# A Strassen form of both network products after the first 512 tokens

## The chip, the cores and the metric

The kernel runs on one core of a Trainium2 chip. The metric is device time in microseconds (us) from start to end of one execution. The engines work side by side, each through its own list of instructions in order: TensorE (PE in the profile; PEld is its weight load) multiplies matrices into PSUM, VectorE (DVE) and ScalarE (ACT) work element by element, GpSimd (POOL) too, though not on PSUM, and SyncE (SP) here only issues transfers (DMA) between DRAM and the on-chip memory. An engine whose next instruction waits does nothing else meanwhile.

## What is computed

```python
def _attn_ref(q, k, v):                      # q, k, v: (8, 8, 576, 64)
    scores = np.matmul(q, k.transpose(0, 1, 3, 2)) / np.sqrt(D)
    # heads 0-3: only the last 32 keys up to the query's own; heads 4-7: keys at distance 0, 32, 64, ...
    scores = np.where(masks[None], scores, -1e9)
    attn = softmax(scores)                   # written out with max, exp and sum + 1e-9
    return np.matmul(attn, v)

def _moe_ref(x, w_in, w_out):                # x (4608, 512), w_in (512, 2048), w_out (2048, 512)
    h = x @ w_in
    g = np.where(h >= 1, h, np.where(h <= -1, 0, (h + 1) ** 2 / 4))
    return g @ w_out
```

x is the attention's output, heads side by side. Everything is float32. The two network products are by far the larger part: 2 x 4608 x 512 x 2048 multiplications.

## The kernel before

Both products are done with operands that are split in a rounded part (high) and the rest (low), as three matmuls for one: high x high, low x high, high x low (HI_LO). A matmul takes a 128x128 block of one operand as weights and moves 512 columns through it. The 4608 tokens are worked in 9 chunks c of 512 (CH). For each chunk the 2048 inner features are worked in 16 tiles f of 128 (NF).

- `up(c, f)` (L540) makes h of tile f: 4 blocks of the 512 inputs times 3, 12 matmuls into one PSUM bank.
- `gate(c, f)` makes g of it: ACT `Relu` and `Square` (L549, L550), DVE min/max (L554), a rounded copy (L556 on ACT, in the first chunk L558 on DVE), and the low part (L559, DVE).
- `down(...)` (L570) multiplies g of one or two tiles with w_out: 12 matmuls a tile, into four PSUM banks that are summed over all 16 tiles; after the last tile ACT copies them out (L577) and SP stores them.

So a chunk is 16 x 24 = 384 matmuls of 512 columns, all nine are 3456. The weights come as pairs of 32-bit words and are converted once, in the first chunk (`conv_a` to `conv_e`: ACT, DVE, POOL, ACT, DVE); after that all 16 tiles lie on chip, split, until the end. The attention of batch b (576 tokens, four units 0 to 3) is spread over the tiles of an earlier chunk by the tables STEPS and LATER, a letter for each step: s scores (PE), m mask and x maximum (DVE), a subtract (POOL), e exponent (ACT), q sum (DVE), p and r normalise, t and j transpose by DVE and a trip through DRAM (or f, a transpose on PE), v values (PE), h and l high and low part of x. The order on each engine is the order in which the code is written. POOL has little beside this: 256-wide and 512-wide sums of the conversion (L191) and the attention's subtract and multiply (L368, L392).

## Time and profile before

| | |
|---|---|
| median of 3 runs | 881.58 us (881.12 to 883.56) |
| span of the profiled execution | 881.9 us |
| PE busy | 872.9 us, 99% |
| ACT busy | 398.0 us, 45% |
| DVE busy | 384.6 us, 44% |
| POOL busy | 114.7 us, 13% |
| DMA | 77.61 MB, 88 GB/s over the span |

The span is the time of the run to within the spread of the runs, so terms read from this trace can be set against the median directly. The page's sections are: busy time by engine; the span in 40 slices; the DMA queues; the chain of work that ended last; the costliest groups of instructions with the idle time before them and what ended it; the DMA issues. Two cautions: durations of neighbouring matmuls overlap, so their spacing is read from start times, and the mean duration of an ACT or DVE instruction also overlaps a little with its neighbour's.

### The profile page before, as it was taken

Reading aid. Unit: us, or ns where it says so; the run is one execution under the profiler, and the core shown is the slowest. Engines: PE = TensorE matmul, PEld = TensorE weight load, DVE = VectorE, ACT = ScalarE, POOL = GpSimd, SP = SyncE. Lnnn points to the kernel's source line nnn. Section 1 sums busy time; section 2 is a strip of 40 time slices with the busy share of each in tenths; the row PEclk is TensorE's granted clock in tenths of the full one; section 3 lists DMA queues with packets and bytes.
Section 4 is the critical chain, followed back from the end, with each engine's and each line's share of the span. In section 5 each row is a group of like instructions: output and inputs, shape, how many; then the busy total and the mean of one; then the engine's idle time right before and its main releaser. Section 6 shows DMA issues by size and latency. Waiting matters only on the chain.

```text
span 881.9 us, 17353 instructions
## 1 busy us (share of the span) xinstructions
PE 872.9 (99%) x7253; PEld 710.3 (81%) x7253; DVE 384.6 (44%) x709; ACT 398.0 (45%) x732; POOL 114.7 (13%) x136
## 2 busy tenths in 40 slices
PE   8999999999999999999999999999999999999998
PEld 6788888888888888887888888888888888888886
DVE  5899854443453434434344345333453322222221
ACT  5889953434434443334434343444333433343333
POOL 6354411100120002100110011100210000000000
PEclk8999999999999999999999999999999999999999
DMA  9917331422232322421241223321222000000001
GB/s 354 405 65 242 114 121 61 140 59 60 105 100 81 83 70 72 125 64 62 81 145 52 67 105 94 87 82 49 76 82 60 33 29 1 0 35 14 1 0 48
DMA packets 41646, 77.61 MB, mean 88 GB/s; under 512 B 8800, under 2 KB 22112, under 8 KB 41568
## 3 DMA queue, kind: packets, MB, share of 16 engines
q1 hardware_dynamic: 41568, 76.50, 26.8%
q8 instruction: 57, 0.93, 0.4%
q14 instruction: 21, 0.17, 0.1%
HBM read 59.18 MB, written 17.30 MB: 87 GB/s over the span
## 4 chain that ended last, share of the span: by engine, by line
PE 95%; DMA 1%; ACT 1%; DVE 1%; SPq 1%; issue 0%; ACTq 0%; DVEq 0%
PE o L570 44%; PE h L540 44%; PE xp L459 3%; PE sc L302 3%; DMA qk<-in_qk_s 1%; PE tp L405 1%; SPq L443 0%; DMA pT<-there 0%; ACT u L549 0%; ACT u L550 0%; DMA there<-t 0%; DVE xTl L504 0%; DVE h L554 0%; SPq L237 0%; ACT gh L556 0%
## 5 line engine op out<-in xcount | busy, mean ns | idle before, releaser
L540 PE MATMUL h<-xTh,w 128*128 128x512 f32 x1152 | 373.2, 391 | 0.4 <-DVE u L554 0.4
L570 PE MATMUL o<-w,gh 128*128 128x512 f32 x1152 | 359.5, 393 | 0.1
L554 DVE SCALAR_TENSOR_TENSOR h<-h,u 128x512 f32<-128x512 f32 x143 | 100.0, 699 | 377.1 <-ACT u L550 377.0
L540 PEld LDWEIGHTS h<-xTh,w 128*128 128x128 f32 x1152 | 216.3, 188 | 46.6 <-DVE u L554 0.8
L570 PEld LDWEIGHTS o<-w,gh 128*128 128x128 f32 x1152 | 213.4, 188 | 45.3 <-ACT gh L556 0.6
L540 PE MATMUL h<-xTl,w 128*128 128x512 f32 x576 | 224.5, 390 | 0.4 <-DVE xTl L504 0.4
L570 PE MATMUL o<-w,gl 128*128 128x512 f32 x576 | 224.9, 390 | 0.0
L549 ACT ACTIVATE u<-h,half 128x512 f32<-128x512 f32 x144 | 99.1, 688 | 269.6 <-PE h L540 268.6
L559 DVE TENSOR_TENSOR gl<-h,gh 128x512 fp32r<-128x512 f32 x143 | 98.9, 692 | 84.6 <-ACT gh L556 83.7
L570 PEld LDWEIGHTS o<-w,gl 128*128 128x128 f32 x576 | 108.1, 188 | 25.7 <-DVE gl L559 0.6
L540 PEld LDWEIGHTS h<-xTl,w 128*128 128x128 f32 x576 | 108.1, 188 | 22.9 <-DVE xTl L504 1.1
L556 ACT CAST gh<-h 128x512 fp32r<-128x512 f32 x128 | 75.2, 587 | 100.1 <-DVE h L554 100.1
L550 ACT ACTIVATE u<-u 128x512 f32<-128x512 f32 x144 | 91.0, 632 | 4.6
L368 POOL TENSOR_TENSOR pr<-pr,st 128x768 f32<-128x768 f32 (+3 forms) x31 | 36.3, 1172 | 322.8 <-DVE st L364 307.6
L392 POOL TENSOR_TENSOR pr<-pr,st 128x648 f32<-128x648 f32 (+3 forms) x30 | 35.2, 1173 | 119.3 <-DVE st L391 118.4
L191 POOL TENSOR_TENSOR raw<-raw 128x512 uint32<-128x512 uint32 (+1 forms) x34 | 35.0, 1047 | 37.9 <-DVE raw L186 23.4
L504 DVE TENSOR_TENSOR xTl<-xp,xTh 128x216 fp32r<-128x216 f32 (+8 forms) x94 | 35.7, 442 | 6.0 <-ACT xTh L500 6.0
L383 ACT ACTIVATE st<-st 128x12 f32<-128x12 f32 (+2 forms) x32 | 6.8, 211 | 67.5 <-DVE st L379 67.4
L459 PEld LDWEIGHTS xp<-pT,v 64*64 64x64 f32 (+2 forms) x1760 | 29.0, 138 | 10.1 <-issue 8.2
L302 PEld LDWEIGHTS sc<-qk 64*32 64x32 f32 (+1 forms) x1856 | 25.9, 117 | 12.1 <-issue 10.1
L459 PE MATMUL xp<-pT,v 64*64 64x32 f32 (+2 forms) x1760 | 32.3, 224 | 1.5 <-DMA pT<-there 0.8
L500 ACT CAST xTh<-xp 128x216 fp32r<-128x216 f32 (+8 forms) x94 | 31.1, 459 | 6.0 <-DVE xTl L504 3.5
(56 smaller groups left out, 348.3 us busy)
## 6 DMA issues: line engine op xcount, KB each, us to landing
raw<-in_w SPq DMA_DIRECT2D x30, 512.0 KB, 9.6
qk<-in_qk_s SPq DMA_DIRECT2D x16, 604.0 KB, 4.9
qk<-in_qk_l SPq DMA_DIRECT2D x16, 576.0 KB, 4.8
out<-ob SPq DMA_DIRECT2D x35, 256.0 KB, 2.0
v<-in_v_l SPq DMA_DIRECT2D x21, 384.0 KB, 4.0
there<-t SPq DMA_DIRECT2D x96, 48.0 KB, 1.7
pT<-there SPq DMA_DIRECT2D x12, 384.0 KB, 3.0
v<-in_v_s SPq DMA_DIRECT2D x7, 384.0 KB, 4.4
```

The lines of the kernel that those rows point to most:

```text
L302: nc.tensor.matmul(sc[j][i * Q:(i + 1) * Q, s, p], qk[:, 0, q0:q0 + Q], qk[:, 1, k0:k0 + W], start=u not in covered, stop=u not in covered)
L368: eng.tensor_tensor(out=pr, in0=pr, in1=st[:, 0].unsqueeze(2).broadcast_to(list(pr.shape)), op=ALU.add)
L392: eng.tensor_tensor(out=pr, in0=pr, in1=st[:, 2].unsqueeze(2).broadcast_to(list(pr.shape)), op=ALU.mult)
L459: nc.tensor.matmul(xp[p][j * D:(j + 1) * D, n], loaded[b, local, b0 + n][keys, j], qs, start=True, stop=True)
L504: nc.vector.tensor_tensor(out=dst[1], in0=src, in1=dst[0].bitcast(F32), op=ALU.subtract)
L540: nc.tensor.matmul(o_ps[c, f], wt[f][:, x, 0, cc * P:(cc + 1) * P], xT[y][:, cc, r0:r0 + CH], start=first and n == 0, stop=last and n == l ...
L549: nc.scalar.activation(u, hp, AF.Relu, bias=half, scale=0.5)
L550: nc.scalar.activation(u, u, AF.Square)
L554: nc.vector.scalar_tensor_tensor(out=g, in0=hp, scalar=1.0, in1=u, op0=ALU.max, op1=ALU.min)
L556: nc.scalar.copy(gh, g)
L559: nc.vector.tensor_tensor(out=gl, in0=g, in1=gh.bitcast(F32), op=ALU.subtract)
L570: nc.tensor.matmul(o_ps[c][t], gs[x][:, t * P:(t + 1) * P], wt[f][:, y, 1, :], start=f == 0 and n == 0, stop=f == NF - 1 and n == 2)
```

## The change

The first 512 tokens are done as before, except that the output is stored transposed (features by tokens; it is turned back outside the device program) and that the down product has the weights as its stationary side. The other 4096 tokens are done in four blocks s of 1024. In a block each product is cut in 2 x 2 by 2 x 2 blocks, and seven products (m = 1 to 7, Winograd's form of Strassen's method) stand in for eight: seven sums and differences of weight blocks, of which three are the blocks themselves, are multiplied with seven of x (or g), and the results are added up in PSUM and by ACT and DVE.

- **Weights.** After its conversion each weight block that is used as it is goes to DRAM (`ship`). `combine(i, j, tag)` makes the four sums of a pair of tiles j (i = 0 for w_in, 1 for w_out): four POOL operations of 256 columns, an ACT copy of 1024 columns, a DVE subtraction of 1024, and one store of 1 MB to DRAM, all by way of one on-chip place called `tag`. Four of the 16 pairs' sums are made beside the first 512 tokens (COMBINE), in four different places. The other twelve are made in the first block of 1024 tokens, two for each j from 0 to 5, after products 1 and 6, all in the place `h2`.
- **Reading back.** From then on each product reads its weights from DRAM: `fetch_w` loads 256 KB for six matmuls, ten ahead (WR).
- **Up.** `up_block` runs 56 units of six matmuls, UP giving the order: for each j products 1, 2, 6, 5, 7, and 3 and 4 one j later. The sum of products grows in the banks y, x, z of one of two sets; between, ACT copies y or z out (g11, g12, g22), DVE adds, and `bent`, `squared` (ACT) and `gated` (DVE) make g. No high and low parts are made here.
- **Down.** `down_block` runs 28 units of twelve matmuls; `prep` makes each unit's sum of g (POOL) and splits it into high and low part (`split`: ACT and DVE, 1024 columns), two units ahead. `x_sum` and `x_split` make the same of x for the next block beside it.
- **Attention.** Batches 1 and 2 are both done beside the first 512 tokens (both by PE transposes; before, batch 2 went through DRAM), 3 and 4 in the up half of the first block, 5 and 6 in the second's, 7 in the third's. x is kept unsplit.

```diff
+    def combine(i, j, tag):
+        def block(r, c):
+            par, h = (r, c) if i == 0 else (c, r)
+            return hts[j][:, par, i, h * HF:(h + 1) * HF]
+        st = slot(tag, [P, 4, 2, HF], F32R, f"st_{i}_{j}")
+        s_ = [st[:, n, 1].bitcast(F32) for n in range(4)]
+        for to, a, b, op in ((0, block(1, 0), block(1, 1), ALU.add), (1, s_[0], block(0, 0), ALU.subtract),
+                             (2, block(0, 0), block(1, 0), ALU.subtract), (3, block(0, 1), s_[1], ALU.subtract)):
+            nc.gpsimd.tensor_tensor(out=s_[to], in0=a, in1=b, op=op)
+        nc.scalar.copy(st[:, :, 0], st[:, :, 1].bitcast(F32))
+        nc.vector.tensor_tensor(out=st[:, :, 1], in0=st[:, :, 1].bitcast(F32), in1=st[:, :, 0].bitcast(F32), op=ALU.subtract)
+        nc.sync.dma_start(kept[i][j][1], st.bitcast(F32))
...
+    UP = [(j - late, m) for j in range(NP + 1) for m, late in ((1, 0), (2, 0), (3, 1), (6, 0), (4, 1), (5, 0), (7, 0)) if 0 <= j - late < NP]
+    DOWN = [(m, k) for m in (1, 2, 6, 7, 5, 3, 4) for k in range(NP // 2)]
...
+    def fetch_w(n):
+        if n < len(seq):
+            i, j, m = seq[n]
+            ring[n] = wr_p.tile([P, 2, HF], F32R, tag="wr", name=f"wr_{n}")
+            which, at = FACTOR[m]
+            nc.sync.dma_start(ring[n].bitcast(F32), kept[i][j][which][:, at])
...
+    def up_block(s, between, prepare):
+        y, x, z, tmp = {}, {}, {}, {}
+        sets = (("b2", "b0", "b1"), ("b3", "b4", "b5"))
+        for n, (j, m) in enumerate(UP):
+            w_ = factor(0, j, m)
...
+                y[j] = bank(at[0], [P, CH], f"y_{s}_{j}")
+                tmp[j] = slot(f"h{jj}", [P, 2, CH], F32, f"tmp_{s}_{j}")
...
+            for c in range(2):
+                for q, (a, b) in enumerate(HI_LO):
+                    nc.tensor.matmul(to, w_[:, a, c * P:(c + 1) * P], xc[m][:, b, c],
+                                     start=m in (1, 2, 5) and c + q == 0, stop=c == 1 and q == 2,
+                                     skip_group_check=m in (3, 4, 6, 7))
+            fetch_w(done - 1 + WR)
...
+            if m == 1:
+                last = (gb[(j - 1) // 2][:, 1, (j - 1) % 2], tmp[j - 1][:, 1]) if j else None
+                if last:
+                    bent(last[1], last[0])
+                nc.scalar.copy(g11, y[j])
+                if last:
+                    squared(last[1])
+                    gated(last[0], *last)
+            elif m == 2:
+                nc.vector.tensor_tensor(out=g11, in0=x.pop(j), in1=g11, op=ALU.add)
+                bent(ua, g11)
+                squared(ua)
...
+            elif m == 6:
+                nc.scalar.copy(g12, y[j])
+                gated(g11, g11, ua)
...
+            elif m == 4:
+                h = y.pop(j)
+                bent(ua, h)
+                squared(ua)
+                gated(g21, h, ua)
...
+            between(n)
...
+    def prep(s, n):
+        if n >= len(DOWN):
+            return
+        m, k = DOWN[n]
+        hl[n] = t = slot(("h2", "h0", "h1")[n % 3], [P, 2, 2, CH], F32R, f"hl_{s}_{n}")
...
+        split(t, {1: b11, 6: b11, 5: t3, 7: t3, 3: b22, 2: b21, 4: b21}[m])
...
-        for c in range(NCH):
...
+        COMBINE = {4: (0, 0, "h1"), 5: (1, 0, "h2"), 6: (0, 1, "h0"), 8: (1, 1, "r7")}
...
+        LATER = {0: ("s0", "m0 x0 a0"), 2: ("", "e0"), 4: ("s1", "m1 x1 a1 q0 p0 r0"), 6: ("", "e1"), 7: ("", "q1 p1 r1"),
+                 9: ("s2", "t0 j0 m2 x2 a2"), 11: ("", "e2"), 13: ("s3", "t1 j1 m3 x3 a3 q2 p2 r2"), 15: ("v0", "e3"),
...
+        for s in range(NSC):
+            batches = [b for b in range(last(s) + 1, B) if s + 1 < NSC and b <= last(s + 1)]
+            def beside(n):
+                j, m = UP[n]
+                if s == 0 and m in (1, 6) and j + 2 < NP:
+                    combine(m // 6, j + 2, "h2")
...
+            up_block(s, beside, lambda m: m in (6, 5) and prep(s, int(m == 5)))
...
+            down_block(s, beside_down)
```

Three places show how the instructions move. First PE: before, one tile's up product in chunk 1 and the start of the down products of the two tiles before it (h, o: PSUM; xTh, xTl: x high and low; w: weights; gh, gl: g).

```order
L540 MATMUL h_1_8_2285<-xTh_153,w_8_1065 128x512
L540 MATMUL h_1_8_2285<-xTl_154,w_8_1065 128x512
L540 MATMUL h_1_8_2285<-xTh_153,w_8_1065 128x512 x2
L540 MATMUL h_1_8_2285<-xTl_154,w_8_1065 128x512
L540 MATMUL h_1_8_2285<-xTh_153,w_8_1065 128x512 x2
L570 MATMUL o_1_0_1941<-w_6_924,gh_1_6_2149 128x512 x2
L570 MATMUL o_1_0_1941<-w_6_924,gl_1_6_2150 128x512
```

Now, in the first block of 1024 tokens, j = 2 and 3 (y, x, z: PSUM, named x_0_2_2631 and so on where they are results; wr: weights read back; in brackets the engines and transfers whose signals the first matmul waits for).

```order
L665 MATMUL z_0_1_2587<-x_0_3_2284,wr_14_2414 128x512 [waits DMAHW6_49,Activation_49]
L665 MATMUL y_0_2_2607<-x_0_6_2242,wr_15_2467 128x512 [waits DMAHW1_49,Activation_49]
L665 MATMUL y_0_1_2459<-x_0_4_2287,wr_16_2488 128x512 [waits DMAHW3_49]
L665 MATMUL z_0_2_2794<-x_0_5_2245,wr_17_2500 128x512 [waits DMAHW4_49]
L665 MATMUL y_0_2_2607<-x_0_7_2237,wr_18_2514 128x512 [waits DMAHW5_49,Activation_49]
L665 MATMUL y_0_3_2834<-x_0_1_1879,wr_19_2534 128x512 [waits DMAHW7_49,DVE_49]
```

A product of six matmuls stands in place of a tile's twelve, and products 3, 6 and 7 wait for ACT (a copy of y or z), product 1 for DVE (the last gate out of the bank that it takes over).

Second, ACT. Before, in chunk 1: two tiles' gates (u, gh of tiles 1 and 2; h: PSUM).

```order
L549 ACTIVATE u_1_1_1872<-h_1_1_1856,half_151 128x512
L550 ACTIVATE u_1_1_1872<-u_1_1_1872 128x512
L556 CAST gh_1_1_1870<-h_1_1_1856 128x512
L549 ACTIVATE u_1_2_1923<-h_1_2_1878,half_151 128x512
L550 ACTIVATE u_1_2_1923<-u_1_2_1923 128x512
L556 CAST gh_1_2_1921<-h_1_2_1878 128x512
```

Now, in the first block of 1024 tokens, from product 1 of j = 2 to its product 6 (ga, gb: the blocks of g; tmp: the gates' u; st_0_4 and st_1_4: the weight sums of pair 4; pr, st_3_2: attention of batch 3).

```order
L675 COPY ga_0_1_2609<-y_0_2_2607 128x512
L560 ACTIVATE tmp_0_1_2460<-tmp_0_1_2460 128x512
L210 CAST st_0_4_2623<-st_0_4_2623 128x4x256
L557 ACTIVATE tmp_0_2_2608<-ga_0_1_2609,half_145 128x512
L560 ACTIVATE tmp_0_2_2608<-tmp_0_2_2608 128x512
L387 ACTIVATE st_3_2_2581<-st_3_2_2581 128x12
L557 ACTIVATE tmp_0_1_2460<-ga_0_0_2292,half_145 128x512
L687 COPY ga_0_1_2609<-y_0_2_2607 128x512
L560 ACTIVATE tmp_0_1_2460<-tmp_0_1_2460 128x512
L210 CAST st_1_4_2719<-st_1_4_2719 128x4x256
```

The casts of the weight sums (L210) stand in ACT's list among the copies and gates of the products.

Third, POOL and SP in the same block. POOL before, in chunk 3: only the attention (pr, st).

```order
L368 TENSOR_TENSOR pr_4_0_3702<-pr_4_0_3702,st_4_0_3703 128x768
L368 TENSOR_TENSOR pr_4_1_3817<-pr_4_1_3817,st_4_1_3818 128x384
L392 TENSOR_TENSOR pr_4_0_3702<-pr_4_0_3702,st_4_0_3703 128x768
L392 TENSOR_TENSOR pr_4_1_3817<-pr_4_1_3817,st_4_1_3818 128x384
L342 MEMSET pr_4_2_3945 128x12x10
```

POOL now, from the first pair's sums (st_0_2, ht: unsplit weights) into the second's (st_1_2, same place).

```order
L209 TENSOR_TENSOR st_0_2_2303<-ht_2_846 128x256 [waits DMAHW5_49,DMAHW1_49,DMAHW6_49,DMAHW0_49,PE_49]
L209 TENSOR_TENSOR st_0_2_2303<-st_0_2_2303,ht_2_846 128x256 [waits Pool_49]
L209 TENSOR_TENSOR st_0_2_2303<-ht_2_846 128x256
L209 TENSOR_TENSOR st_0_2_2303<-ht_2_846,st_0_2_2303 128x256 [waits Pool_49]
L372 TENSOR_TENSOR pr_3_0_2361<-pr_3_0_2361,st_3_0_2362 128x768 [waits DVE_49]
L209 TENSOR_TENSOR st_1_2_2389<-ht_2_846 128x256 [waits DMAHW1_49,Activation_49]
```

SP now, at the same place (ks: the sums in DRAM, kq: the blocks in DRAM).

```order
L612 DMA wr_10_2300<-ks_0_1_153 128x512 [waits DMAHW0_49,PE_49]
L212 DMA ks_0_2_155<-st_0_2_2303 128x2048 [waits DMAHW1_49,DVE_49]
L612 DMA wr_11_2374<-ks_0_1_153 128x512 [waits DMAHW2_49,PE_49]
L612 DMA wr_12_2385<-kq_0_2_154 128x512 [waits DMAHW3_49,PE_49]
L212 DMA ks_1_2_171<-st_1_2_2389 128x2048 [waits DMAHW4_49,DVE_49]
L612 DMA wr_13_2405<-kq_0_2_154 128x512 [waits DMAHW5_49,PE_49]
```

SP issues the store of the first sums on the signal DMAHW1, and that is the signal for which POOL waits before it writes the second sums to the same place; the reads of weights stand behind the stores in SP's list.

More of the change, by code (lines that the diff above doesn't have):

```diff
@@ new lines, in squared, with gated, gate @@
+    def squared(u):
+        nc.scalar.activation(u, u, AF.Square)
+    def gated(to, h, u):
+        nc.vector.scalar_tensor_tensor(out=to, in0=h, scalar=1.0, in1=u, op0=ALU.max, op1=ALU.min)
+    def gate(f, between=lambda: None):
+        hp = o_ps.pop(f)
+        u, gh, gl = (wr_p.tile([P, CH], t, tag="wr", name=f"{n}_{f}") for n, t in (("u", F32), ("gh", F32R), ("gl", F32R)))
+        bent(u, hp)
+        squared(u)
+        between()
+        g = u if f == 0 else hp
+        gated(g, hp, u)
+        nc.vector.tensor_copy(gh, g)
@@ new lines, in down @@
+    def down(f, gs):
+        if f == 0:
+            o_ps["o"] = [psum("o", [P, CH], f"o_{d}") for d in range(NC)]
+        for d in range(NC):
+            c, e = divmod(d * P, HF)
+            for n, (x, y) in enumerate(HI_LO):
+                nc.tensor.matmul(o_ps["o"][d], wt[f][:, 1, c, x, e:e + P], gs[y],
+                                 start=f == 0 and n == 0, stop=f == NF - 1 and n == 2)
+            if f == NF - 1:
+                ob = o_p.tile([P, CH], F32, tag="ob", name=f"ob_{d}")
+                nc.scalar.copy(ob, o_ps["o"][d])
+                put(d, 0, ob)
@@ L614, in tile_sparse_attention_then_ffn @@
         load_w(2, 0)
[L615 removed]
+        for f in range(3):
+            load_w(f, 1)
+        for i in range(2):
+            load_w(3, i)
         for p in range(2):
             load_qk(1, p)
[L618 removed]
+        for f in (4, 5):
+            for i in range(2):
+                load_w(f, i)
         begin("""
```

420 lines of the change are left out of this document (273 added, 147 removed), and 7 rows, old and new, of tables (LATER, STEPS).

## The prediction

> **What bounds the kernel now.** I read the page's busy times and slices first, then the chain of waits, then the costliest groups.
>
> ```profile
> span 881.9 us, 17353 instructions
> PE 872.9 (99%) x7253; PEld 710.3 (81%) x7253; DVE 384.6 (44%) x709; ACT 398.0 (45%) x732; POOL 114.7 (13%) x136
> ...
> PEclk8999999999999999999999999999999999999999
> DMA  9917331422232322421241223321222000000001
> GB/s 354 405 65 242 114 121 61 140 59 60 105 100 81 83 70 72 125 64 62 81 145 52 67 105 94 87 82 49 76 82 60 33 29 1 0 35 14 1 0 48
> ...
> PE 95%; DMA 1%; ACT 1%; DVE 1%; SPq 1%; issue 0%; ACTq 0%; DVEq 0%
> ...
> L540 PE MATMUL h<-xTh,w 128*128 128x512 f32 x1152 | 373.2, 391 | 0.4 <-DVE u L554 0.4
> L570 PE MATMUL o<-w,gh 128*128 128x512 f32 x1152 | 359.5, 393 | 0.1
> ```
>
> PE is busy for 872.9 of 881.9 us, at full clock after the first slice, and holds 95% of the chain. Its two products wait for nothing (0.4 and 0.1 us). So PE work is the time, until something makes PE wait. The span is 0.3 us above the median of 881.58 us: I forecast against the span and call the two the same.
>
> The price of a matmul comes from start times, since mean durations overlap. PE's timeline in chunk 7 has 24 up matmuls between the first and the second row, 24 of down between the second and the third:
>
> ```profile
> 694.63 0.39 PE L540 MATMUL h<-xTh,w 128*128 128x512 f32 x1
> ...
> 700.08 0.61 PE L570 MATMUL o<-w,gh 128*128 128x512 f32 x2
> ...
> 705.55 0.39 PE L540 MATMUL h<-xTh,w 128*128 128x512 f32 x1
> ```
>
> 48 in 10.92 us: 0.2275 us each, 1.365 us for a unit of six. Windows by stage (load, first chunk, second, eighth, and the middle of the first):
>
> ```profile
> core 0: us, PE busy (x) PEld busy (x) DVE busy (x) ACT busy (x) POOL busy (x), PEclk, DMA share, GB/s
> 0.00:27.00 27.00, 23.31 (x537) 18.59 (x537) 16.43 (x36) 15.01 (x39) 15.18 (x35) 0.87 0.95 364
> 27.00:124.36 97.36, 96.61 (x947) 77.50 (x945) 83.33 (x152) 81.69 (x154) 40.99 (x41) 1.00 0.51 183
> 124.36:220.37 96.01, 96.01 (x850) 78.32 (x849) 40.19 (x80) 39.10 (x77) 9.74 (x10) 1.00 0.28 85
> 701.34:793.00 91.66, 91.66 (x405) 75.17 (x404) 23.65 (x34) 35.18 (x57) 0.00 (x0) 1.00 0.05 18
> 30.31:117.86 87.55, 87.19 (x817) 70.58 (x816) 77.54 (x142) 76.96 (x145) 40.99 (x41) 1.00 0.49 176
> ```
>
> The first chunk is the only one where ACT and DVE are nearly full (84 and 86%). The second, with one batch of attention, takes 96.0 us; its 384 wide matmuls are 87.4, so a batch costs PE 8.6.
>
> **The change part by part.**
>
> *PE work.* Before, 9 x 384 = 3456 wide matmuls. After, 384 for the first 512 tokens, and for each of four blocks 56 x 6 + 28 x 12 = 672, in all 3072. 384 fewer x 0.2275 = **-87.4 us**. Batch 2 is now transposed on PE too: 20 more of a group that has 40 in 6.9 us,
>
> ```profile
> L405 PE MATMUL tp<-ident,pr 128*128 128x128 f32 x40 | 6.9, 318 | 0.6 <-DVE pr L392 0.6
> ```
>
> which is **+3.4**. If PE never waited, the end would be 881.9 - 87.4 + 3.4 = 797.9. The question is what PE waits for.
>
> *The sums of the weights in the first block's up half.* This is the largest term. Twelve sums go through the one place h2. POOL may not write the next until the store of the last has landed; ACT's copy (L210) waits for POOL; and ACT's list has that copy in the midst of the copies and gates for which products 3, 6 and 7 wait on PE, while DVE's subtraction stands ahead of gates for which product 1 waits. So a late sum stops ACT, and ACT stops PE. What a sum takes is POOL, ACT, DVE and store one after the other. The nearest rows, by form:
>
> ```profile
> L191 POOL TENSOR_TENSOR raw<-raw 128x256 uint32<-128x256 uint32 x4 | 2.8, 709 | 7.2 <-DVE raw L186 5.4 <-ACT raw L178 1.8
> L368 POOL TENSOR_TENSOR pr<-pr,st 128x768 f32<-128x768 f32 x8 | 11.8, 1476 | 239.1 <-DVE st L364 224.0 <-PE o L570 14.9 <-DMA raw<-in_w 0.2
> L368 POOL TENSOR_TENSOR pr<-pr,st 128x384 f32<-128x384 f32 x8 | 6.7, 831 | 62.6 <-DVE st L364 62.6
> L197 ACT CAST w<-raw 128x512 fp32r<-128x512 f32 x29 | 18.9, 667 | 4.2 <-POOL raw L191 3.9
> L197 ACT CAST w<-raw 128x256 fp32r<-128x256 f32 x4 | 1.6, 423 | 0.2
> L201 DVE TENSOR_TENSOR w<-raw,w 128x512 fp32r<-128x512 f32 x30 | 19.4, 684 | 0.0
> L201 DVE TENSOR_TENSOR w<-raw,w 128x256 fp32r<-128x256 f32 x4 | 1.5, 417 | 0.0
> ```
>
> - POOL: four operations of 256 columns, 4 x 0.709 = 2.84. From the f32 rows at 768 and 384 columns the slope gives 0.62 for 256, so 2.46 as the lower end. I take 2.84, a row of that very width.
> - ACT, 1024 columns: 0.667 + 2 x (0.667 - 0.423) = 1.16. DVE: 0.684 + 2 x (0.684 - 0.417) = 1.22.
> - The store of 1 MB, of which before has none. Its stores of 256 KB and loads of 512 KB, from the DMA issues and the answer on the tile raw:
>
> ```profile
> raw<-in_w SPq DMA_DIRECT2D x30, 512.0 KB, 9.6
> qk<-in_qk_s SPq DMA_DIRECT2D x16, 604.0 KB, 4.9
> out<-ob SPq DMA_DIRECT2D x35, 256.0 KB, 2.0
> ...
> DMA to landing us min/median/max: 2.9/9.5/11.1
> ```
>
> 256 KB land in 2.0 and 512 KB at best in 2.9, so 0.9 more for each 256 KB: 4.7 for 1 MB. Lower: 2.0 and 0.79 MB at the 405 GB/s of the busiest slice, 3.95; lowest, it lands like the best 512 KB, 2.9. Upper: behind other transfers, as the loads of 604 KB need 4.9 and those of 512 KB 9.6 in a full queue; about 7.1 in the middle of these.
>
> The sum: 2.84 + 1.16 + 1.22 + 4.7 + 0.1 of handing over = 10.0, and I add 0.5 for transfers ahead in the queue: 10.5 (7.8 by the lowest ends, 12.9 by the upper). One step j of the up half has two sums, so 21.0 us, where PE has only 7 x 1.365 = 9.56 and 2.15 of attention. So the stage is paced by the sums: eleven sums in full, 11 x 10.5 = 115.5; the twelfth up to DVE's end 5.3; a gate 0.7; then 16 units not yet done, 21.8; attention still to come, 5.9; small waits 3. Together 152.2. PE has 56 x 1.365 = 76.4 and two batches, 17.2: 93.6. So **+58.5**. The transfers themselves would fit: 12.6 MB of sums, 14.7 of weights read back and 7.4 of attention are 35 MB in 152 us, 230 GB/s where 364 and 405 were seen.
>
> The Trainium skill, "DMA: Bandwidth & Descriptors", section "Anatomy of one DMA — SWDGE (gpsimd) path", has a figure of about 2.0 us fixed and 436 GB/s. By it, as an estimate, 1 MB lands in 4.4 and the stage would be some 3 us shorter; it would also give 2.6 for 256 KB, where the trace has 2.0, so I keep the rows.
>
> *First 512 tokens.* A second batch and four sums join ACT (77.0 of 87.55 us in the middle window) and DVE (77.5). By the second chunk less the eighth a batch is 16.5 us of DVE (40.19 - 23.65) and 3.9 of ACT; four sums are 4.9 and 4.6; of the batch's DVE work the low parts of x fall away,
>
> ```profile
> L504 DVE TENSOR_TENSOR xTl<-xp,xTh 128x216 fp32r<-128x216 f32 (+8 forms) x94 | 35.7, 442 | 6.0 <-ACT xTh L500 6.0
> ```
>
> 35.7 / 8 = 4.5. So DVE comes to 94 and ACT to 86 or more, in a stage of some 99 us (87.5 and 12 of PE for the batch): DVE is 95% full. The stage's transfers were 183 GB/s x 97.4 us = 17.8 MB; shipped blocks add 12.6, four sums 4.2, the first ten reads 2.6: 37 MB, which at 364 to 405 GB/s takes 92 to 102 us. Both are at the edge: **+5** (0 to 10).
>
> *Up halves of blocks 2 to 4.* There is one loop of ACT and DVE left: product 4's result goes through Relu, Square and the gate before product 1 of two steps later may start in that bank.
>
> ```profile
> L549 ACT ACTIVATE u<-h,half 128x512 f32<-128x512 f32 x144 | 99.1, 688 | 269.6 <-PE h L540 268.6
> L550 ACT ACTIVATE u<-u 128x512 f32<-128x512 f32 x144 | 91.0, 632 | 4.6
> L554 DVE SCALAR_TENSOR_TENSOR h<-h,u 128x512 f32<-128x512 f32 x143 | 100.0, 699 | 377.1 <-ACT u L550 377.0
> ```
>
> 0.69 + 0.63 + 0.70 = 2.02, and two units of PE, 2.73, lie between. What attention puts in front on ACT or DVE is not covered: I take 6 for the second block, with two batches, and 2 each for the third and fourth: **+10** (0 to 25). If the cover were gone, the loop would cost up to 2.0 in each of 24 steps, 48.
>
> *Down halves.* A unit is 12 x 0.2275 = 2.73 us and its split (1.16 on ACT, 1.22 on DVE) is issued two units ahead, so it is hidden; copies and sums where accumulators change cost some 0.75 a block: **+3**.
>
> The sum: 881.9 - 87.4 + 3.4 + 58.5 + 5 + 10 + 3 = 874.4. **Forecast 874.**
>
> **The rivals.**
>
> *Rival 1, short sums.* The stores land like the best 512 KB and POOL runs at its lower end: 7.84 a sum, so 11 x 7.84 + 36.7 = 123, +29.3 in place of +58.5: 845. For it: the queues are half empty in the mean. Against: a store of 1 MB has never been seen here.
>
> *Rival 2, stores that queue (the other side).* Place: the transfer from h2 to DRAM. Each store has up to ten weight reads and the loads of two batches for company, as the 512 KB loads had when they took 9.6. At 7.1 a store, 12.9 a sum: 11 x 12.9 + 36.7 = 178.6, +85: 901. It decides from 0.9 us more per sum than I take (11.4 in all): then the kernel is slower than 884.2. For it: 0.95 DMA share in the load stage, when transfers crowd. Against: 230 GB/s in the mean.
>
> *Rival 3, the gate's loop.* Work of attention ahead of the gate costs 1 us more in each of the 24 steps, 898 from the sum. For it: ACT and DVE work in order. Against: DVE is about 82 of 94 us full only in the second block.
>
> *Rival 4, the clock.* PEclk is 0.87 in the first 27 us, where PE has gaps, and 1.00 after. If it halves in waits of 7 to 9 us each step, the work between waits is slower; PE work of 93.6 us would take 187, which beats the chain of sums by 35: 909. The Trainium skill, "TensorE: Matmul & The Clock Gate", section "Part 1: The HAM clock gate (the "warmup" mystery)", tells of such a halving after a few microseconds of idling; the trace agrees as far as 0.87 goes, no run here shows it within a stage. Against: in most steps the slower work would lie within the wait.
>
> **How the numbers follow.** Forecast 0.50, rival 1 0.17, rival 2 0.20, rival 3 0.08, rival 4 0.05. About 0.3% (878.9 and 884.2) is what can be told from no change. The forecast's own range is 862 to 890, since one sum's 1 us moves it by 11: within it faster 0.29, same 0.09, slower 0.12. With rival 1 faster comes to 0.46; rivals 2 to 4, nearly all slower, bring slower to 0.42; same 0.12. The range of 8 in 10 reaches half way into rival 1 and over rival 2's middle: 850 to 903.
>
> **What would show it.** In the profile after: POOL's first operation of a sum (L209) idle until the store ks has landed, ACT's copy L210 idle until POOL, and PE's L665 idle 7 to 9 us a step until ACT, in the first block alone; steps of some 21 us there; ks landing in about 5 us; the first up half near 152 us, later ones 95 to 100, 85 and 78, down halves near 78; PE with 3072 wide matmuls, still 0.2275 us apart. I am wrong if the first up half is near 94 us (the sums hidden), if the later up halves wait as much as the first, if ks lands in under 3 or over 7 us, or if PEclk falls below full in the later stages.

## The result, and the profile after

The changed kernel takes 1060.99 us (median of 4 runs, 1056.91 to 1062.54), the kernel before in the same comparison 882.17 us: a ratio of 1.2015, 95% interval 1.1985 to 1.2046. The forecast was 874, its range 850 to 903. The span of the profiled execution is 1059.2 us.

The page of the changed kernel: busy times, slices, the chain of waits, and two groups.

```profile
span 1059.2 us, 18019 instructions
...
PE 868.3 (82%) x6889; PEld 678.7 (64%) x6889; DVE 660.3 (62%) x771; ACT 520.0 (49%) x855; POOL 411.2 (39%) x278
...
PE   8766678766466779899678689799998979999998
...
PEclk9898879887767989999969799899999989999999
DMA  9946955666666776566666766376676647666563
...
PE 37%; DVE 23%; ACT 11%; DMA 9%; POOL 5%; issue 4%; SPq 1%; DVEq 0%; ACTq 0%; POOLq 0%
...
L637 DVE TENSOR_TENSOR hl<-ga,hl 128x1024 fp32r<-128x1024 f32 x64 | 149.6, 2361 | 34.8 <-ACT hl L636 34.7
```

PE held 95% of the chain before and holds 37% now. Its matmuls are fewer, yet it is busy about as long (868.3 us against 872.9), at a granted clock that is below full in many slices. DVE, which the forecast had as a bystander outside the first stage, holds 23%, and its largest single group there is the split of g in the down halves, 2.36 us an instruction.

The windows of the changed kernel, cut where PE goes from one half of a block to the next (load; first 512 tokens; then up and down of each of the four blocks). Columns: length; busy time of each engine; granted clock of PE; share of the DMA engines' time; GB/s.

```profile
core 0: us, PE busy (x) PEld busy (x) DVE busy (x) ACT busy (x) POOL busy (x), PEclk, DMA share, GB/s
0.00:27.00 27.00, 22.58 (x541) 16.94 (x541) 17.93 (x40) 16.67 (x50) 15.16 (x35) 1.00 0.95 365
27.00:196.38 169.38, 124.47 (x1343) 97.19 (x1342) 107.17 (x176) 89.45 (x173) 74.75 (x69) 0.87 0.67 241
196.38:388.79 192.41, 122.09 (x1265) 92.60 (x1264) 89.40 (x136) 82.07 (x139) 66.12 (x72) 0.80 0.66 219
388.79:479.43 90.64, 82.18 (x337) 64.57 (x336) 75.10 (x41) 40.00 (x47) 53.65 (x17) 0.96 0.60 186
479.43:617.45 138.02, 107.20 (x1266) 83.21 (x1265) 68.92 (x121) 66.19 (x129) 27.68 (x23) 0.88 0.67 209
617.45:708.10 90.65, 82.22 (x337) 64.55 (x336) 75.17 (x41) 39.99 (x47) 53.65 (x17) 0.96 0.60 185
708.10:801.69 93.59, 88.81 (x801) 70.01 (x800) 51.85 (x87) 58.89 (x105) 17.79 (x13) 0.98 0.69 220
801.69:895.20 93.51, 82.97 (x338) 64.46 (x336) 77.93 (x43) 40.13 (x44) 54.66 (x17) 0.96 0.57 172
895.20:973.94 78.74, 77.05 (x337) 62.85 (x336) 37.80 (x55) 52.49 (x87) 7.22 (x3) 1.00 0.66 197
973.94:1059.20 85.26, 78.77 (x337) 62.33 (x335) 58.98 (x36) 34.12 (x38) 40.52 (x13) 0.99 0.54 170
```

Set against the stages that the forecast's terms make (27 + 97.4 + 12 + 5 for the first 512 tokens; 93.6 + 58.5; 76.4 and 0.75 for a down half; 93.6 + 6, 76.4 + 8.6 + 2 and 76.4 + 2 for the later up halves):

| stage | forecast, us | measured, us | difference |
|---|---|---|---|
| first 512 tokens, with the load | 141 | 196.4 | +55 |
| up half of block 1 | 152 | 192.4 | +40 |
| up half of block 2 | 100 | 138.0 | +38 |
| up half of block 3 | 87 | 93.6 | +7 |
| up half of block 4 | 78 | 78.7 | 0 |
| down halves 1 to 4 | 309 | 360.1 | +51 |

The one stage that has no attention, no sums of weights and no sums by POOL worth the name, the up half of block 4, came out as forecast. So the plain matmul term holds, and the 191 us that the forecast did not have lie in the other stages (7 us of the forecast had no stage). The experiments take these stages in turn.

The waits in the up half of block 1 (who, for whom: us in all, times, longest), and SP's own there:

```profile
ACT st L210 <- POOL st L209: 41.7, 11, 8.3
...
PE y L665 <- DVE gb L563: 24.6, 6, 6.1
POOL st L209 <- DMA ks<-st: 23.6, 6, 11.3
PE xp L463 <- DMA pT<-there: 22.6, 4, 8.5
...
PE y L665 <- ACT ga L675: 11.2, 3, 6.2
...
PE y L665 <- ACT ga L687: 6.0, 3, 2.4
```

```profile
SPq L212 <- DVE st L211: 60.7, 10, 9.5
```

Of the signs that I had named, two are there: POOL waits for the store (in 6 of 11 cases) and ACT for POOL. The third is there in part: PE waits for ACT's copies only some 17 us in the whole stage, not 7 to 9 us in each of its 8 steps; more of its 70 us go to DVE's gate (24.6). A fourth is there that I had not named: PE waits 22.6 us for pT, the attention's trip through DRAM. SP stands 60.7 us at the stores of the sums with the reads of weights behind it in its list, but the view has no wait of PE for such a read, so that is not what holds PE. The stores of 1 MB land in 4.9 us, the forecast's 4.7:

```profile
wr<-ks SPq DMA_DIRECT2D x256, 256.0 KB, 3.6
wr<-kq SPq DMA_DIRECT2D x192, 256.0 KB, 3.4
...
ks<-st SPq DMA_DIRECT2D x16, 1024.0 KB, 4.9
```

### The profile page after: what moved, and what is told of

It reads as the page before. It is cut to its first block, busy times and chain, and to the rows that moved or that the text cites. A ratio compares the mean times of both kernels' runs of the same rounds, so it can differ in the third digit from the quotient of the medians.

```text
span 1059.2 us, 18019 instructions
## 1 busy us (share of the span) xinstructions
PE 868.3 (82%) x6889; PEld 678.7 (64%) x6889; DVE 660.3 (62%) x771; ACT 520.0 (49%) x855; POOL 411.2 (39%) x278
## 4 chain that ended last, share of the span: by engine, by line
PE 37%; DVE 23%; ACT 11%; DMA 9%; POOL 5%; issue 4%; SPq 1%; DVEq 0%; ACTq 0%; POOLq 0%
DVE hl L637 12%; PE yo L768 9%; PE y L665 8%; PE zo L768 6%; PE z L665 4%; DMA ks<-st 3%; POOL st L209 3%; ACT tmp L557 3%; ACT tmp L560 3%; PE x L665 2%; DVE x L637 2%; DMA wr<-kq 2%; PE xo L768 2%; DVE pr L357 2%; PE xp L463 1%
## 5 line engine op out<-in xcount | busy, mean ns | idle before, releaser
L665 PE MATMUL y<-x,wr 128*128 128x512 f32 x768 | 214.7, 425 | 52.1 <-DVE gb L563 28.4
L665 PEld LDWEIGHTS y<-x,wr 128*128 128x128 f32 x768 | 151.9, 203 | 96.4 <-DVE gb L563 33.7
L768 PE MATMUL yo<-hl,wr 128*128 128x512 f32 x768 | 180.3, 392 | 5.0 <-DVE hl L637 4.4
L637 DVE TENSOR_TENSOR hl<-ga,hl 128x1024 fp32r<-128x1024 f32 x64 | 149.6, 2361 | 34.8 <-ACT hl L636 34.7
L768 PEld LDWEIGHTS yo<-hl,wr 128*128 128x128 f32 x768 | 142.8, 188 | 40.6 <-DVE hl L637 10.0
L768 PE MATMUL zo<-hl,wr 128*128 128x512 f32 x384 | 100.6, 423 | 20.1 <-DVE hl L637 20.0
L768 PEld LDWEIGHTS zo<-hl,wr 128*128 128x128 f32 x384 | 78.2, 206 | 41.9 <-DVE hl L637 24.8
L665 PE MATMUL z<-x,wr 128*128 128x512 f32 x384 | 103.8, 407 | 0.6 <-ACT gb L701 0.5
L637 DVE TENSOR_TENSOR hl<-gb,hl 128x1024 fp32r<-128x1024 f32 x48 | 88.5, 1860 | 19.1 <-ACT hl L636 19.0
L463 PEld LDWEIGHTS xp<-pT,v 64*64 64x64 f32 (+2 forms) x1720 | 35.7, 157 | 76.4 <-issue 57.9
L560 ACT ACTIVATE tmp<-tmp 128x512 f32<-128x512 f32 x128 | 80.9, 632 | 2.3
```

The source lines that it names most:

```text
L463: nc.tensor.matmul(xp[p][j * D:(j + 1) * D, n], loaded[b, local, b0 + n][keys, j], qs, start=True, stop=True)
L560: nc.scalar.activation(u, u, AF.Square)
L637: nc.vector.tensor_tensor(out=t[:, 1], in0=src, in1=t[:, 0].bitcast(F32), op=ALU.subtract)
L665: nc.tensor.matmul(to, w_[:, a, c * P:(c + 1) * P], xc[m][:, b, c], start=m in (1, 2, 5) and c + q == 0, stop=c == 1 and q == 2, skip_grou ...
L768: nc.tensor.matmul(to, w_[jj][:, a, d * P:(d + 1) * P], t[:, b, jj], start=m in (1, 2, 5) and k + jj + q == 0, stop=k == NP // 2 - 1 and j ...
```

## The experiments

Each run below is one execution timed and one profiled, beside the kernel before at 880.8 to 881.6 us. The stage of the first 512 tokens took 196.4 us in the changed kernel and 203.3 in runs 2 and 3, whose work there is the same, so differences under some 7 us in that stage say nothing. Rows of the view by windows have the columns given above.

### 1. No sums of weights

```diff
-            which, at = FACTOR[m]
+            which, at = 0, FACTOR[m][1] % 3
-            if f in COMBINE:
-                combine(*COMBINE[f])
-                if s == 0 and m in (1, 6) and j + 2 < NP:
-                    combine(m // 6, j + 2, "h2")
```

> None of the 16 weight sums is made or stored; products 3, 5, 6 and 7 read plain weight blocks in their place, as many bytes, so the result is not the reference's. Theory A, that the sums by way of one place pace the first up half (10.5 us each by POOL, ACT, DVE and store): the first up half falls from 192 us to that of the second, about 138, and the first 512 tokens lose the waits of four sums, some 25 of 196; in all about 980. Theory B, that crowded transfers pace it: 16.8 of 221 MB are gone, the first up half falls by some 10 us only, in all about 1045.

Measured: 992.83 us. The up half of block 1 by windows:

```profile
186.11:328.03 141.92, 107.47 (x1265) 82.94 (x1264) 72.63 (x124) 70.47 (x128) 28.35 (x24) 0.89 0.64 207
```

It falls from 192.4 to 141.9 us, near the 138.0 of block 2; the first 512 tokens to 186.1. So the twelve sums cost 50 us where they stand, and B (10 us) falls. How they cost it, this run does not say.

### 2. Transposes by PE in the up halves

```diff
-                 9: ("s2", "t0 j0 m2 x2 a2"), 11: ("", "e2"), 13: ("s3", "t1 j1 m3 x3 a3 q2 p2 r2"), 15: ("v0", "e3"),
-                 17: ("", "h0 t2 j2 q3 p3 r3"), 22: ("v2", "t3 h2 j3"), 26: ("V1", "h1 h3")}
+                 8: ("f0", "d0"), 9: ("s2", "m2 x2 a2"), 10: ("v0",), 11: ("", "e2 h0"), 12: ("f1", "d1"),
+                 13: ("s3", "m3 x3 a3 q2 p2 r2"), 14: ("v1",), 15: ("", "e3 h1"), 17: ("", "q3 p3 r3"),
+                 18: ("f2", "d2"), 20: ("v2",), 21: ("", "h2"), 22: ("f3", "d3"), 24: ("v3",), 26: ("", "h3")}
```

> In the up halves the attention is transposed by PE, as beside the first 512 tokens, and no longer by way of DRAM; each value product comes two or more units after its transposes. Theory A, that the trip through DRAM, squeezed into 4 to 6 units of 1.4 us, is late and PE waits for it: the second up half falls from 138 to about 108 (23 us of waits for pT gone, slow clock after them too, 7 of PE work more); the first falls by 10 to 20 only, since the sums pace it; the third stays within 4; in all about 1020. Theory B, that the trip hides in other waits: PE's 60 or so transposes come on top and the whole is 1065 or more.

Measured: 1034.76 us. Beside the lines shown, the loads of v are issued after the same steps as beside the first 512 tokens. The up halves of blocks 1 and 2:

```profile
203.28:374.80 171.52, 119.91 (x1306) 92.24 (x1305) 87.70 (x134) 81.14 (x137) 65.54 (x72) 0.84 0.66 221
...
469.22:586.46 117.24, 107.27 (x1305) 83.82 (x1304) 66.88 (x119) 64.90 (x127) 27.51 (x23) 0.94 0.66 206
```

Both fall by 21 us (192.4 to 171.5, 138.0 to 117.2), though PE has 40 small transposes more in each; block 3, where one batch has the whole half and the trip twice the time, stays (94.9). A's place is right, its size for block 2 was some 9 us too large. The whole gains 26 us, not 41, since the down halves got 7 us longer (367.3 against 360.1), which this run does not explain, and the first 512 tokens 7, within the spread. In the changed kernel the wait for pT is 23.0 of the 30.8 us that PE waits in the up half of block 2. Where the trip comes late shows in the timeline of the changed kernel, block 2:

```profile
523.13 7.05 SPq L447 DMA_DIRECT2D there<-t  x8
531.56 0.34 SPq L448 DMA_DIRECT2D pT<-there  x1
...
534.90 1.56 PE L463 MATMUL xp<-pT,v 54*64 54x64 f32 x48 [9.84 <-DMA pT<-there]
```

The eight stores take 7.05 us to be issued alone, the load back goes out 8.4 us after the first of them, and PE's product waits 9.84 us. In the table of steps trip and product stand 4 to 6 units apart, 5.5 to 8.2 us of PE.

### 3. and 4. The sums in the down halves: left out, and by DVE

The third kernel leaves POOL's sums of g and x out; the fourth makes them on DVE.

The third, in `prep` (there the sums of products 4 and 2 too) and beside the down half:

```diff
-        if m == 5:
-            nc.gpsimd.tensor_tensor(out=t3, in0=b22, in1=b11, op=ALU.subtract)
...
-                    do(m, s + 1)
+                    if do is not x_sum:
+                        do(m, s + 1)
```

The fourth, in `x_sum` and for each sum of `prep`:

```diff
-        nc.gpsimd.tensor_tensor(out=to, in0=a, in1=b, op=op)
+        nc.vector.tensor_tensor(out=to, in0=a, in1=b, op=op)
...
-            nc.gpsimd.tensor_tensor(out=t3, in0=b22, in1=b11, op=ALU.subtract)
+            nc.vector.tensor_tensor(out=t3, in0=b22, in1=b11, op=ALU.subtract)
```

> POOL's sums of g and x beside the down halves are left out (the splits take the unsummed blocks, so the result is not the reference's); DVE's and ACT's splits and PE's work stay. Theory A, that DVE's subtraction of two blocks in SBUF and a POOL operation exclude each other: every split takes 1.21 us on DVE (now 2.36 and 1.86 in the mean), and down halves fall from 91, 91, 94 and 85 to 78 each, in all about 1015. Theory B, that the splits are slow by transfers or by ACT's order: their mean stays above 1.8 and the down halves stay above 88, in all above 1045.

> The same sums of g and x are made, but by DVE in place of POOL. Theory A (the two engines exclude each other): DVE takes 1.21 us for a sum where POOL took 2.4 and held DVE off, so DVE has 28 + 17 operations of 1.21 us, 55 of some 78 us: splits at 1.21, down halves at 78 to 81, in all 1015 to 1025. Theory B (DVE as such has too much to do there): with POOL's work added the down halves get longer than 91, in all above 1061.

Measured: 1015.57 and 1032.71 us. The down half of block 1, third then fourth kernel:

```profile
392.07:468.41 76.34, 76.34 (x338) 62.99 (x336) 44.58 (x41) 40.30 (x48) 2.41 (x1) 1.00 0.70 221
```

```profile
391.62:473.18 81.56, 78.23 (x338) 62.59 (x336) 62.05 (x57) 40.44 (x49) 2.41 (x1) 1.00 0.64 207
```

The answer on the line of the splits (ns, least, median and most), in the changed kernel and in the third:

```profile
L637 DVE TENSOR_TENSOR hl<-ga,hl x64: 1209/2399/3427, 379.0 to 1026.4; 128x1024 fp32r<-128x1024 f32 x64
```

```profile
L637 DVE TENSOR_TENSOR hl<-ga,hl x64: 1214/1226/1267, 382.5 to 981.0; 128x1024 fp32r<-128x1024 f32 x64
```

Without POOL every split takes 1.21 to 1.27 us and the half runs at PE's pace, 76.3 us, which is 28 units of 2.73. With the same sums on DVE the splits stay at 1.22 and the half takes 81.6, though DVE has more to do (57 operations for 41). So it is not DVE's load but POOL's operations that lengthen DVE's. The timeline of the changed kernel shows how:

```profile
409.63 1.21 DVE L637 TENSOR_TENSOR hl<-gb,hl 128x1024 fp32r<-128x1024 f32 x1
409.86 3.25 POOL L633 TENSOR_TENSOR xr<-xr 128x1024 f32<-128x1024 f32 x1 [2.36 <-DVE x L637]
...
410.77 3.42 DVE L637 TENSOR_TENSOR hl<-ga,hl 128x1024 fp32r<-128x1024 f32 x1
...
423.30 2.40 POOL L633 TENSOR_TENSOR xr<-xr 128x1024 f32<-128x1024 f32 x1 [4.58 <-DVE x L637]
```

Alone, POOL's takes 2.40 and DVE's 1.21. Overlapping, POOL's takes 3.25: some 1.0 of waiting for the DVE operation that began 0.23 us earlier, then about its own. DVE's next begins while POOL's runs, ends 1.08 us after it, and is told as 3.42. They take turns.

### 5., 6., 12. and 13. The first 512 tokens

Fifth: no attention of batch 2 there. Sixth: three quarters of the stores of blocks left out. Twelfth: no attention of either batch. Thirteenth: as the fifth, with batch 1's steps at every second tile.

The fifth (in the twelfth the condition is `b in (1, 2)`; `plain_x` sets x to 0.5):

```diff
+        if b == 2:
+            steps = dict.fromkeys(steps, lambda u: None) | {"h": plain_x}
```

The sixth, in `ship` and `fetch_w`:

```diff
+        if j > 1:
+            return
...
-            nc.sync.dma_start(ring[n].bitcast(F32), kept[i][j][which][:, at])
+            nc.sync.dma_start(ring[n].bitcast(F32), kept[i][j if which else j % 2][which][:, at])
```

The thirteenth, on top of the fifth (the first two splits of x also stand three tiles later):

```diff
-            b = 1 + (f > 7)
-            steps = STEPS.get(f - 7 * (b - 1), ("",) * 6)
+            b = 1
+            steps = STEPS.get((f + 1) // 2, ("",) * 6) if f % 2 and f < 14 else ("",) * 6
```

> The attention of batch 2 is left out beside the first 512 tokens (its x is set to 0.5, its loads stay), so the result is not the reference's. Theory A, that the steps of two batches in 14 tiles make a loop through PE, ACT, DVE and POOL that takes some 10.5 us a tile where PE has 6.8: the first 512 tokens take 145 to 155 us in place of 196 (12 of it are PE's own work), in all about 1015. Theory B, that the stores of weight blocks and sums hold the conversion up: only PE's work goes, 185 or more, in all about 1048.

> Only the blocks of the first two of eight pairs of tiles go to DRAM (3.1 of 12.6 MB); later reads of a plain block take the block of one of these pairs, so the result is not the reference's. Theory A (loop of two batches): the first 512 tokens stay within 10 of 196 us, in all about 1055. Theory B (stores): they fall to 170 or less, in all about 1030.

> The attention of batches 1 and 2 is left out beside the first 512 tokens (x set to 0.5, loads stay; the result is not the reference's); conversion, stores and four sums stay. Theory A, that the steps of attention, a batch in 7 tiles in place of a batch in 16, make the loop through PE, ACT, DVE and POOL of 10 to 15 us a tile: all tiles take the 5.3 us that tiles 8 to 15 took without batch 2, the stage some 125 to 135 us in place of 196. Theory B, that in tiles 3 to 7 it is the conversion, the stores or the sums: these tiles stay above 9 us each and the stage above 150.

> Batch 2 is left out beside the first 512 tokens as before, and the seven steps of batch 1 stand at every second tile (1, 3, ... 13) in place of tiles 1 to 7; the first two splits of x three tiles later. The same work as in the run without batch 2, where the stage took 164 us. Theory A (too many steps of attention in too few tiles): about 140. Theory B (each step costs its latency wherever it stands, or the cause lies elsewhere): 160 or more.

Measured: 1026.60, 1064.18, 999.90 and 1024.15 us in all. The stage, in this order:

```profile
0.00:164.39 164.39, 136.06 (x1398) 107.29 (x1398) 107.54 (x185) 99.97 (x195) 78.13 (x96) 0.88 0.82 307
```

```profile
0.00:198.85 198.85, 146.82 (x1881) 114.27 (x1882) 125.88 (x215) 106.07 (x221) 89.69 (x104) 0.89 0.58 207
```

```profile
0.00:132.51 132.51, 116.52 (x913) 92.54 (x914) 98.46 (x155) 93.88 (x175) 71.95 (x86) 0.92 1.00 375
```

```profile
0.00:160.69 160.69, 126.14 (x1397) 100.04 (x1398) 113.36 (x186) 102.27 (x199) 85.89 (x100) 0.92 0.84 308
```

Stores are not it: 9.4 MB less changed nothing beyond the spread. Each batch costs some 32 us (196.4, 164.4, 132.5; up to 39 for batch 2 by the upper end of the spread), of which PE's own work is 12. That is A in part. Without attention, transfers fill the DMA engines for the whole stage (share 1.00, 375 GB/s), so 132 us is about the floor for its 50 MB, and batch 1 by itself may cost more than the difference to that floor. The tiles that have a sum of weights still took 9 to 10 us there, from one tile's first Relu to the next's, the others 4 to 6.5; A had 5.3 for all.

Where PE waits after the load, in the changed kernel:

```profile
PE tp L409 <- POOL pr L396: 20.9, 4, 11.9
...
PE xp L463 <- DVE pT L419: 8.2, 3, 4.5
...
PE sc L306 <- ACT xr L510: 6.6, 2, 5.0
```

These and the smaller ones are all 45 us that PE waits in this stage, and every one stands before a matmul of the attention: the transposes wait for POOL's multiply, the value products for DVE's copy of the transposes, the next scores for ACT's copy of the last values. Without batch 2 (the fifth) they are 23 us, without both (the twelfth) none is left. So PE waits at the attention's steps. Spreading batch 1's steps over twice as many tiles, where A expected 140, gave 160.7 in place of 164.4. PE's waits at these steps stayed (21.8 us for 23.3), so it is not how densely they stand that makes them; that each step costs its own latency fits this, but was not tested by itself. The 160.7 are not the whole of it: at the end PE waits 7.7 us for the first weights read back (wr<-kq), which the fifth does not have. Without that the stage would have taken some 153 (an estimate), the gain lying in PE's busy time after the load, 104.0 for 114.1, at a granted clock of 0.90 for 0.85. Why a step of attention waits here and not in the first chunk of the kernel before, which has one batch and where PE waits for next to nothing (96.6 us busy of 97.4), these runs do not settle.

### 7. The one place as two halves

`st` is now made once for the twelve sums, and in `combine` (so for the four sums beside the first 512 tokens too) stands:

```diff
-        for to, a, b, op in ((0, block(1, 0), block(1, 1), ALU.add), (1, s_[0], block(0, 0), ALU.subtract),
-                             (2, block(0, 0), block(1, 0), ALU.subtract), (3, block(0, 1), s_[1], ALU.subtract)):
-            nc.gpsimd.tensor_tensor(out=s_[to], in0=a, in1=b, op=op)
...
+        for n, todo in ((0, ((0, block(1, 0), block(1, 1), ALU.add), (1, s_[0], block(0, 0), ALU.subtract))),
+                        (2, ((2, block(0, 0), block(1, 0), ALU.subtract), (3, block(0, 1), block(1, 1), ALU.subtract),
+                             (3, s_[3], s_[2], ALU.add)))):
+            for to, a, b, op in todo:
+                nc.gpsimd.tensor_tensor(out=s_[to], in0=a, in1=b, op=op)
+            part = st[:, n:n + 2]
+            nc.scalar.copy(part[:, :, 0], part[:, :, 1].bitcast(F32))
+            nc.vector.tensor_tensor(out=part[:, :, 1], in0=part[:, :, 1].bitcast(F32), in1=part[:, :, 0].bitcast(F32), op=ALU.subtract)
+            nc.sync.dma_start(kept[i][j][1][:, n:n + 2], part.bitcast(F32))
```

> In the first up half the one place is used as two halves of two sums, each with its own ACT, DVE and store of 512 KB (one POOL operation more, so that a half needs nothing of the other). Theory A, that the wait for the whole store in one place paces this stage: a half takes POOL 1.5 to 2.2, ACT 0.7, DVE 0.7 and a store of 3 to 3.5, some 6.5 us in place of 10.5, the next sum's first half starts under the second's store, and the stage falls from 192 to about 150 us, in all about 1020. Theory B, that the work of the sums in ACT's, DVE's and POOL's order is what costs, not the place: the stage stays above 180, in all above 1048.

Measured: 1066.19 us. The stage:

```profile
204.63:395.87 191.24, 125.86 (x1266) 95.22 (x1265) 96.73 (x148) 83.76 (x151) 79.03 (x84) 0.80 0.66 221
```

191.2 us for 192.4: nothing, though POOL's wait for the store halved there, from 23.6 to 11.9 us. ACT waits for POOL as long as before (41.7 there, 40.8 here):

```profile
ACT st L218 <- POOL st L216: 40.8, 19, 5.9
...
POOL st L216 <- DMA ks<-st: 11.9, 4, 9.4
```

The step on which the largest term of the forecast rested, that the wait for the store in one place paces the stage, falls; B is left. The halves also bring work of their own (POOL is busy 79.0 us in place of 66.1, DVE 96.7 in place of 89.4), so a small gain may be hidden in this.

### 8. Three changes together

The edits 2, 4 and 7 in one kernel.

> Transposes by PE in the up halves, the sums of g and x by DVE and the halves together; the whole is computed. If the three costs add up (26 and 28 us measured, some 40 expected of the halves, the first up half losing its trips through DRAM as well): 960 to 975, still some 9% slower than before, with the first 512 tokens at 196 to 203 us. If they hide one another: above 990.

Measured: 994.78 us. The up half of block 1:

```profile
201.23:369.59 168.36, 118.22 (x1305) 90.04 (x1304) 99.12 (x149) 82.96 (x149) 78.56 (x82) 0.84 0.67 222
```

26 and 28 us add up to 54, and 66 were gained (single runs): the costs do not hide one another, though the total is above 990. What is missing is what I had expected of the halves, which are worth little here too: 168.4 us against 171.5 with PE's transposes alone.

### 9. and 10. The sums later in ACT's and DVE's lists, and made by DVE

Both on top of the eighth.

The ninth (what stands in `due` is issued once unit n + 2 has been: ACT's copy, DVE's subtraction, the store):

```diff
-                    combine(m // 6, j + 2, "h2")
+                    combine(m // 6, j + 2, "h2", due.setdefault(n + 2, []))
```

The tenth, in `combine`:

```diff
-                nc.gpsimd.tensor_tensor(out=s_[to], in0=a, in1=b, op=op)
+                (nc.vector if j > 1 else nc.gpsimd).tensor_tensor(out=s_[to], in0=a, in1=b, op=op)
```

> On top of the three changes of the run before (first up half 168 us there): ACT's copy, DVE's subtraction and the store of a sum stand two units of six matmuls later in the lists than POOL's part. Theory C, that ACT waits for POOL's sum in the midst of the copies and gates that PE needs (31 us of ACT's idle time there), because POOL's list has the attention's operations ahead of the sum: the first up half falls from 168 to about 145. Theory D, that the work of the sums on ACT and DVE is what costs, wherever it stands: it stays above 160.

> On top of the same three changes: the twelve sums of the first up half are made by DVE in place of POOL (five operations of 0.42 us in place of 0.74, nothing of them in POOL's list). Theory C: 31 us of ACT's waits for POOL go, 25 us of DVE's work come, the first up half falls from 168 to about 150. Theory D: DVE's list gets longer and the stage with it, 168 or more.

Measured: 988.61 and 1020.49 us. The stage in each:

```profile
201.91:360.69 158.78, 117.31 (x1306) 90.17 (x1304) 95.28 (x149) 82.19 (x149) 76.40 (x82) 0.86 0.70 236
```

```profile
204.04:393.00 188.96, 127.86 (x1306) 98.05 (x1304) 114.55 (x209) 83.85 (x149) 27.75 (x23) 0.78 0.60 199
```

Later: 158.8, between the two theories. ACT's wait for POOL falls from 31.0 to 14.2 us there, but POOL's wait for the store rises from 6.9 to 18.7, since the store now goes out later too. By DVE: 189.0, worse by 21, and ACT now waits 45.9 us for DVE. PE's longest waits there:

```profile
PE sc L316 <- DVE pT L429: 30.0, 4, 12.8
```

That is DVE's copy of the attention's transposes; for the gates PE waits 5.2 us. So where a sum's work stands decides, and of the three places tried DVE's list is the worst, since what PE waits for next is in that list. The ninth is the fastest of these kernels that compute the whole, 12% above the kernel before.

### 11. The second and fourth edit, and no sums of weights

The edits 1, 2 and 4 in one kernel.

> Transposes by PE in the up halves and the sums of g and x by DVE as before, and none of the 16 weight sums is made (products 3, 5, 6 and 7 read plain blocks, so the result is not the reference's). If the sums cost what they did with the trips through DRAM (50 us), the first up half falls from 168 to that of the second, 118, and the first 512 tokens from 201 to about 186; in all about 927, still above the kernel before, and the 186 us of the first 512 tokens stay as what is left over.

Measured: 930.08 us. The first 512 tokens and the up half of block 1:

```profile
0.00:177.29 177.29, 144.15 (x1882) 111.85 (x1882) 123.23 (x213) 102.86 (x217) 68.06 (x84) 0.92 0.73 263
177.29:301.35 124.06, 108.43 (x1305) 84.16 (x1304) 72.84 (x125) 69.19 (x125) 27.52 (x23) 0.94 0.63 199
```

The sums cost 44 us in the up half (168.4 to 124.1) and 10 to 25 beside the first 512 tokens. With trips, POOL's sums and weight sums all gone the kernel is still 49 us above the kernel before, and 36 of that is what the first 512 tokens need above the forecast's 141.

## Why the prediction was wrong

- **PE's work (-87.4).** Right. The number of wide matmuls and their price hold: a down half without disturbance is 76.3 us, the last up half 78.7 for 78.4.
- **Sums of weights (+58.5).** The parts of the price were right: POOL's four operations 3.2 us (0.84, 0.84, 0.76 and 0.73 in the mean), ACT 1.05, DVE 1.36, the store 4.9, 10.5 in all, as forecast. The cost was near too, 50 us by taking them out. The mechanism was not: "the stage is paced by the sums" through the store in the one place failed (run 7), so that 58.5 stands near 50 is luck. What the runs leave is that a sum's work stands in ACT's, DVE's and POOL's lists ahead of what PE waits for (runs 9 and 10). Moving ACT's and DVE's part gave back 10 of 44 us; the other 34 are not split further. The stage missed by 40 all the same, 21 of it by the attention's trips, which I had counted as so much work of PE ("two batches, 17.2") with no latency.
- **First 512 tokens (+5, 0 to 10).** The worst step. I added busy times, found DVE 95% full and the transfers near their limit, and put 5 us on that. Every engine works in order, and no engine was full: after the load DVE was busy 107 of 169 us (for the 94 of my sum, which left out 5.3 of splits of x), and PE waited 45, all of it at the attention's steps and 21 for POOL, which my sum did not have at all. PE was also busy 124.5 us where its work was priced at 109, at a granted clock of 0.87. A second batch was priced at PE's 12 us and cost 32, sums at nothing beyond DVE's and ACT's busy time and cost 10 to 25. The stage's transfers after the load were 41 MB for the 37 forecast, and did not bound it (share 0.67).
- **Up halves 2 to 4 (+10, 0 to 25).** I looked at one loop only, the gate of product 4, and gave 6 us to block 2. It cost 38: 21 went with the trips through DRAM (run 2), and of the 18 left then some 7 are the transposes that PE does in their place. That the trip has 4 to 6 units there and twice as many in block 3 stood in the table of steps, which I had quoted and not timed.
- **Down halves (+3).** The prediction's step was "issued two units ahead, so it is hidden". The split's 1.21 us alone was as forecast (1.22); beside a POOL operation it was 2.4 to 3.4. POOL's sums have no term in the prediction at all: I had not asked what POOL and DVE share. Cost: 48 us of the 51 (run 3).
- **The rivals.** None held. Rival 1 had the store at 2.9 us and rival 2 at 7.1; it was 4.9. Rival 3's gate before product 1 made PE wait under 4 us in the three later up halves together, where it needed 24. Rival 4's mechanism is there, the clock was below full in every stage with long waits, but I put it in one stage only. The range failed since its upper end let one term go wrong at a time. Four of them did, all one way, and three for one reason: work was priced by busy time wherever the engine's share of the stage left room. The fourth, the down halves, failed on what two engines share.

## What to carry to other kernels

When a step is moved into a shorter stage, price it by the time from its first instruction to the one that PE waits for, through every in-order list and every trip through DRAM, and compare that with the units of PE between; a free share of an engine is no cover. Before calling work on an idle engine free, look in the trace for what its operations do to a neighbour's: POOL's sums here cost DVE more than DVE would have spent on making them itself. And take a supposed bottleneck away in a run before building on it: the store in the one place gave nearly the right price by the wrong cause.

## What the runs showed of the hardware

**DVE and POOL take turns.** A DVE subtraction of two blocks in SBUF and a POOL operation on SBUF do not overlap: 1.21 and 2.40 us alone, 3.42 and 3.25 when they meet, and 1.21 to 1.27 always when POOL is taken out. The Trainium skill, "SBUF — State Buffer", section "Who interferes with whom", states that a DVE instruction with two SBUF inputs contends with a GpSimd instruction that reads SBUF, and that this contention is an exclusive lock; the trace agrees, with these numbers. Read beside this change it would have pointed at the down halves' term, though it has no size for it.

**The granted clock is lower where PE waits.** It was 0.80 in the up half of block 1 (PE waits 70 of 192 us), 0.87 and 0.88 in the first 512 tokens and block 2, 1.00 in the last up half and in the down halves of run 3. PE's work of 93.6 us was told as 122.1 busy in the first of these. The answer on the up products gives single matmuls from 387 to 796 ns:

```profile
L665 PE MATMUL y<-x,wr x768: 387/389/796, 196.4 to 973.7; 128*128 128x512 f32 x192
```

The Trainium skill, "TensorE: Matmul & The Clock Gate", section "Part 1: The HAM clock gate (the "warmup" mystery)", tells of half rate after idling; the largest is about twice the least here, so the trace agrees as far as that goes. How much of the time the slower clock added, beyond filling waits that were there anyway, no run told apart.
